# The segment loop of a recurrent memory transformer: hand-computed waits in one hardware loop, and ring loads of one row

## The chip, the cores and the metric

The kernel runs on one core of a Trainium2 chip. The metric is the device time of one execution in microseconds (us), as the median of five runs. In the profile the engines are called PE (TensorE, matrix products), DVE (VectorE), ACT (ScalarE), POOL (GpSimd) and SP (SyncE, which only issues transfers here). PEld is TensorE's weight load.

## The reference, cut to what matters

The output is two halves side by side, each 2048 x 640. The left half (part A) is an attention over eight earlier positions with a stride of two. The right half (part B) is a transformer layer with memory, and the change touches only this. It cuts the 2048 rows into 64 segments of 32, and each segment is worked on together with eight rows of memory, which the segment before has produced:

```python
mem = mem0                                   # 8 x 640
for s in range(64):
    h = concatenate([mem, x[32*s : 32*s+32]])        # 40 x 640
    q, k, v = h @ Wq, h @ Wk, h @ Wv                 # 32 heads of 192
    p = softmax(where(mask, q @ k.T * scale, -1e9))  # 40 x 40 for each head
    o = (p @ v) @ Wo                                 # 40 x 640
    mem = o[:8]
    out[s] = o[8:]
```

The memory makes the segments sequential: no projection of a segment can begin before the output projection of the one before is done. All data are bf16 and the sums are float32.

## The kernel before

Part A (line 24 on) runs first, in 16 blocks. Part B (`part_b`, line 150 on) then computes everything that does not depend on the memory: the last eight rows of each segment, the "left" rows, are projected for all segments at once (lines 223 to 283) and kept in DRAM (`qk_scr`, `v_scr`). What is left for the loop is 32 rows a segment: 24 of the input and 8 of memory.

The four weight matrices are cut into 64 units of 128 x 1920 (480 KB): 16 each for Q, K and V, and 16 for the output (O). 44 units are resident in the on-chip buffer. The other 20, about every third in the order of use, are streamed: each segment loads them anew from DRAM into a ring of five buffers (`load_ring`, line 339), a load being issued as soon as TensorE is through with the unit five before it. After 20 loads the ring begins again for the next segment.

A segment runs through these steps, in the order of the calls at the end of `segment`:

- 12 projections (`proj`, line 372), four each for Q, K and V. Each is 20 matmuls: five slices of the model's width by four groups of heads, the groups at four column positions of the array. HT, the transposed input of the segment, is the weight operand.
- A cast out of PSUM (line 380; ACT for Q, DVE for K), six transposes (`turn`, line 396) and a copy into QT or KT (line 399).
- `scores` for half of the heads (line 417, 32 small matmuls), and the softmax behind it: scale and mask (422), maximum (426), subtraction (427) and sum (430), reciprocal (431) and the products P and PL (433, 434) on DVE, and exp (428) on ACT.
- `turn_p` transposes P (451, 453), `pv` multiplies with V (469 to 484), and four casts bring the result into OT (487, alternately ACT and DVE).
- `oproj`: 16 output units of 12 matmuls each (line 500), all summed up in one PSUM tile Y.
- At the end DVE forms z, the next segment's input, from Y and the next x rows (537), and transposes it into HT (538). ACT copies Y to yo (541), and this goes out (542).

The work of TensorE and SyncE stands in the order in which the code is written (`manual_schedule`, line 547). For the other engines a scheduler orders the instructions, and tile pools give out the buffers. The 64 segments are four hardware loops of 16 iterations (lines 548 to 550), each with `iteration_sync="barrier"`: at the end of an iteration all engines drain, the semaphores are set back, and only then does any engine go on. Behind the loops, the left rows get their output projection (line 581).

Of the kernel before, what the change touches and what calls it, by code (L numbers as in the profile page):

```python
# [7 lines left out]
FP32 = mybir.dt.float32  # L8
BF16 = mybir.dt.bfloat16
ALU = mybir.AluOpType  # L10
# [138 lines left out]

def part_b(ctx, tc, B_x, B_mem0, B_Wq, B_Wk, B_Wv, B_Wo, out, ident, run_a):  # L150
# [24 lines left out]
    N_STR, N_RING, N_LOOPS = 20, 5, 4  # L175
# [21 lines left out]
    ws_scr = {u: dram.tile([128, US], BF16, name=f"ws_{u[0]}_{u[1]}_{u[2]}") for u in streamed}  # L197
    xz_scr = dram.tile([n_seg + 2, 4, 32, 160], BF16, name="xz_scr")
    qk_scr = dram.tile([n_seg + 1, 128, 2, 48 * NL], BF16, name="qk_scr")
    v_scr = dram.tile([n_seg + 1, 128, 2 * Dh], BF16, name="v_scr")  # L200
    ol_scr = dram.tile([n_seg, 128, 48 * NL], BF16, name="ol_scr")
# [89 lines left out]
    psum = lctx.enter_context(tc.tile_pool(name="b_ps", bufs=8, space=PSUM))  # L291

    def acc(shape, dt=FP32, name="acc"):
        return psum.tile(shape, dt, tag="acc", name=name)
# [24 lines left out]
    QTW = 24 * L  # L319
    PLs = [cst.tile([128, 4, 4, NL], BF16, name=f"PL{t}") for t in range(2)]  # L320
# [8 lines left out]
    def load_left(s):  # L329
        nc.sync.dma_start(qkl[:].rearrange("p t c j l -> p t (c j l)"), qk_scr[s])  # L330

    def load_vl(s):
        nc.sync.dma_start(vl[:].rearrange("p e n -> p (e n)"), v_scr[s])

    def load_x(s):
        nc.sync.dma_start(xz[:], xz_scr[s].rearrange("g t n -> (g t) n"))  # L336

    def load_ring(k):
        nc.sync.dma_start(ws_ring[k % N_RING][:], ws_scr[streamed[k % N_STR]][:])  # L339

    z0 = one.tile([128, 160], BF16, tag="z")
# [4 lines left out]
    load_left(0)  # L346
    load_vl(0)
    load_x(1)
    for k in range(N_RING):
        load_ring(k)  # L350
    pos = {u: k for k, u in enumerate(streamed)}
# [3 lines left out]

    def done(us):
        for u in us:
            if u in pos:
                load_ring(pos[u] + N_RING)

    def segment(s):
        cur = {"QT": None, "KT": None}
        nat = {}
        P = [None, None]
        PTs = [None, None]

        def proj(ty, r):
            ps = acc([128, 384], name="pj")
            ws = [get((ty, r, j)) for j in range(4)]
            for dc in range(5):  # L370
                for j in range(4):
                    nc.tensor.matmul(ps[32 * j:32 * j + 32, :], lhsT=HT[:, dc, :], rhs=ws[j][:, dc, :],  # L372
                                     start=(dc == 0), stop=(dc == 4), tile_position=(0, 32 * j))
            done([(ty, r, j) for j in range(4)])
            return ps

        def qk(ty, r):
            ps = proj(ty, r)
            n_ = two.tile([128, 384], BF16, tag="nat", bufs=3, name="nat")
            (nc.scalar.copy if ty == Q else nc.vector.tensor_copy)(n_[:], ps[:])  # L380
            nat[ty, r] = n_

        def turn(r):
            t = r // 2
            if r % 2 == 0:
                QT = cur["QT"] = one.tile([128, QTW + 24], BF16, tag="qt", name="QT")
                KT = cur["KT"] = one.tile([128, QTW], BF16, tag="kt", name="KT")
                nc.gpsimd.memset(QT[:, QTW:QTW + 24], 0.0)
                for T_, ty in ((QT, Q), (KT, K)):
                    nc.gpsimd.tensor_copy(T_[:, 0:QTW].rearrange("p (c j l) -> p c j l", c=6, j=4)[:, :, :, 32:L],  # L390
                                          qkl[:, ty, 6 * t:6 * t + 6])
            tp = acc([128, 2, 3, 4, 32], BF16, name="tp")
            for ty in (Q, K):
                n_ = nat.pop((ty, r))
                for c in range(3):
                    nc.tensor.transpose(tp[:, ty, c].rearrange("p j l -> p (j l)"), n_[:, 128 * c:128 * c + 128], ident)  # L396
            for T_, ty in ((cur["QT"], Q), (cur["KT"], K)):
                dst = T_[:, 0:QTW].rearrange("p (c j l) -> p c j l", c=6, j=4)[:, 3 * (r % 2):3 * (r % 2) + 3, :, 0:32]
                (nc.scalar.copy if ty == Q else nc.vector.tensor_copy)(dst, tp[:, ty])  # L399

        def scores(t):
            QT, KT = cur["QT"], cur["KT"]
            Sps = acc([128, 8, L], name="S")
# [11 lines left out]
            for n, (_, lo, rr, j, e, cc, hi) in enumerate(pl):  # L415
                o = (4 * cc + j) * L
                nc.tensor.matmul(Sps[64 * e:64 * e + 64, 4 * rr + j, :], lhsT=QT[lo:hi, o:o + 64],  # L417
                                 rhs=KT[lo:hi, o:o + L], start=(e not in seen), stop=(n == last[e]),
                                 tile_position=(lo, 64 * e))
                seen.add(e)  # L420
            t1 = two.tile([128, 8, L], FP32, tag="t1", name="t1")
            nc.vector.scalar_tensor_tensor(out=t1[:], in0=Sps[:], scalar=scale,
                                           in1=mask[:].unsqueeze(1).to_broadcast([128, 8, L]),
                                           op0=ALU.mult, op1=ALU.add)
            mx = two.tile([128, 8], FP32, tag="mx", name="mx")
            nc.vector.tensor_reduce(out=mx[:], in_=t1[:], axis=AX.X, op=ALU.max)
            nc.vector.tensor_tensor(t1[:], t1[:], mx[:].unsqueeze(2).to_broadcast([128, 8, L]), op=ALU.subtract)
            nc.scalar.activation(t1[:], t1[:], ACTF.Exp)  # L428
            sm = two.tile([128, 8], FP32, tag="sm", name="sm")
            nc.vector.tensor_reduce(out=sm[:], in_=t1[:], axis=AX.X, op=ALU.add)  # L430
            nc.vector.reciprocal(sm[:], sm[:])
            P[t] = two.tile([128, 8, 32], BF16, tag="P", name="P")
            nc.vector.tensor_tensor(P[t][:], t1[:, :, 0:32], sm[:].unsqueeze(2).to_broadcast([128, 8, 32]), op=ALU.mult)
            nc.vector.tensor_tensor(PLs[t][:, :, 2 * t:2 * t + 2, :].rearrange("p j r k -> p r j k"),
                                    t1[:, :, 32:L].rearrange("p (r j) k -> p r j k", r=2),
                                    sm[:].rearrange("p (r j) -> p r j", r=2).unsqueeze(3).to_broadcast([128, 2, 4, NL]),
                                    op=ALU.mult)

        Vn = one.tile([128, 4, 2, Dh], BF16, tag="V")

        def vproj(r):
            ps = proj(V, r)
            (nc.scalar.copy if r % 2 else nc.vector.tensor_copy)(Vn[:, r].rearrange("p e n -> p (e n)"), ps[:])

        OTs = [None, None]
# [213 lines left out]
```

## Time and profile before

| | us |
|---|---|
| median of 5 runs | 3211.32 (3204.09 to 3217.65) |
| profiled execution | 3215.68 |
| its span, first to last instruction | 3211.4 |
| busy in the span: PE | 1965.9 (61%) |
| PEld | 1202.3 (37%) |
| DVE | 992.8 (31%) |
| ACT | 612.3 (19%) |
| POOL | 164.4 (5%) |

The busy time of an engine is summed over the whole span. The program has three stages with different limits: part A and the left projections up to about 733 us, the 64 segments up to 3133 us, and the tail. A mean over all three tells little on any of them. The clock that TensorE was granted was 0.84 on the mean; 1.00 stands for 2.4 GHz and 0.50 for 1.2.

### The profile page before, as it was taken

Reading aid. Unit: us, or ns where it says so; the run is one execution under the profiler, and the core shown is the slowest. Engines: PE = TensorE matmul, PEld = TensorE weight load, DVE = VectorE, ACT = ScalarE, POOL = GpSimd, SP = SyncE. Lnnn points to the kernel's source line nnn. Section 1 sums busy time; section 2 is a strip of 40 time slices with the busy share of each in tenths; the row PEclk is TensorE's granted clock in tenths of the full one; section 3 lists DMA queues with packets and bytes.
Section 4 is the critical chain, followed back from the end, with each engine's and each line's share of the span. In section 5 each row is a group of like instructions: output and inputs, shape, how many; then the busy total and the mean of one; then the engine's idle time right before and its main releaser. Section 6 shows DMA issues by size and latency. Waiting matters only on the chain. (4 is left out here: it accounts for less than half of the span.)

```text
span 3211.4 us, 98839 instructions
## 1 busy us (share of the span) xinstructions
PE 1965.9 (61%) x42567; PEld 1202.3 (37%) x42592; DVE 992.8 (31%) x2357; ACT 612.3 (19%) x1494; POOL 164.4 (5%) x572
## 2 busy tenths in 40 slices
PE   0017868761466667666676666666676666666667
PEld 0004543330244344434444344444443344434444
DVE  0015652210133333333333333333333233333330
ACT  0012222210122122212122122212221122212221
POOL 0000100000000000000000000000000000000000
PEclk9998989885688787888889888887888888878888
DMA  4347754443688788887788787787888778877885
GB/s 132 109 139 255 260 205 131 149 134 108 214 303 308 259 287 290 285 287 272 281 297 309 268 286 283 279 292 272 303 290 286 270 274 293 306 283 282 287 298 181
DMA packets 360652, 806.41 MB, mean 251 GB/s; under 512 B 54432, under 2 KB 186720, under 8 KB 360592
## 3 DMA queue, kind: packets, MB, share of 16 engines
q1 hardware_dynamic: 333876, 764.98, 67.9%
q0 software_dynamic: 5984, 26.67, 2.3%
q10 hardware_dynamic: 20732, 13.93, 1.4%
q8 instruction: 41, 0.67, 0.1%
q14 instruction: 19, 0.16, 0.0%
HBM read 765.54 MB, written 51.80 MB: 255 GB/s over the span
## 5 line engine op out<-in xcount | busy, mean ns | idle before, releaser
L372 PE MATMUL pj<-w,HT 128*32 128x384 bf16 x10560 | 915.6, 383 | 492.7 <-PEq L549 463.4
L372 PE MATMUL pj<-ring,HT 128*32 128x384 bf16 x4800 | 925.1, 383 | 248.7 <-DMA ring<-ws 246.8
L372 PEld LDWEIGHTS <-HT 128*32 128x32 bf16 x15360 | 441.9, 109 | 1078.9 <-issue 732.5
L380 DVE CAST nat<-pj 128x384 bf16<-128x384 f32 x256 | 141.3, 552 | 715.7 <-PE pj L372 705.9
L380 ACT CAST nat<-pj 128x384 bf16<-128x384 f32 x256 | 122.7, 479 | 1195.7 <-PE pj L372 1101.8
L500 PEld LDWEIGHTS <-OT 128*32 128x32 bf16 x12288 | 240.2, 100 | 171.3 <-issue 122.8
L500 PE MATMUL Y<-w,OT 128*32 128x160 bf16 x8448 | 243.5, 242 | 13.7 <-issue 9.7
L500 PE MATMUL Y<-ring,OT 128*32 128x160 bf16 x3840 | 132.4, 245 | 105.3 <-DMA ring<-ws 99.0
L399 DVE COPY KT<-tp 128x384 bf16<-128x384 bf16 x256 | 91.6, 358 | 295.7 <-ACT QT L399 294.7
L399 ACT COPY QT<-tp 128x384 bf16<-128x384 bf16 x256 | 122.4, 478 | 140.4 <-PE tp L396 140.3
L396 PE MATMUL tp<-ident,nat 128*128 128x128 bf16 x1536 | 144.1, 236 | 0.2 <-DVE nat L380 0.2
L58 PE MATMUL pT<-ident,xb 128*128 128x128 bf16 x80 | 8.1, 236 | 213.4 <-DMA xb<-in_A_x_dram 210.4
L396 PEld LDWEIGHTS <-nat 128*128 128x128 bf16 x1536 | 96.1, 104 | 100.3 <-issue 99.9
L417 PE MATMUL S<-KT,QT 128*64 128x40 bf16 (+1 forms) x4096 | 120.4, 187 | 0.0
L417 PEld LDWEIGHTS <-QT 128*64 128x64 bf16 (+1 forms) x4096 | 103.4, 110 | 44.7 <-issue 40.7
L487 DVE CAST OT<-ot 128x240 bf16<-128x240 f32 x256 | 95.4, 393 | 58.8 <-PE ot L484 58.8
L430 DVE TENSOR_REDUCE sm<-t 128x8 f32<-128x320 f32 x128 | 61.9, 484 | 148.3 <-ACT t L428 146.4
L278 PE MATMUL ps<-t,XL 128*128 128x384 bf16 x320 | 70.6, 371 | 49.2 <-DMA t<-in_B_Wv_dram 47.4
L537 DVE SCALAR_TENSOR_TENSOR z<-Y,rows,xz 128x160 bf16<-128x160 f32 x64 | 24.6, 384 | 238.8 <-PE Y L500 238.8
L487 ACT CAST OT<-ot 128x240 bf16<-128x240 f32 x256 | 78.9, 360 | 101.6 <-PE ot L484 101.3
L65 PE MATMUL pq<-wqkv,xT 128*128 128x480 bf16 x320 | 87.0, 400 | 16.9 <-ACT xT L60 10.0
L488 POOL COPY olt<-OT 128x192 bf16<-128x192 bf16 x128 | 44.7, 349 | 896.5 <-DVE OT L487 896.5
(103 smaller groups left out, 1921.1 us busy)
## 6 DMA issues: line engine op xcount, KB each, us to landing
ring<-ws SPq DMA_DIRECT2D x1285, 480.0 KB
K<-a_kv_scr SPq DMA_DIRECT2D x16, 1280.0 KB
V<-a_kv_scr POOLq DMA_DIRECT2D x16, 1280.0 KB, 9.4
qkl<-qk_scr SPq DMA_DIRECT2D x65, 192.0 KB
qk_scr<-st SPq DMA_DIRECT2D x4, 3072.0 KB
t<-ws SPq DMA_DIRECT2D x25, 480.0 KB
v_scr<-vs SPq DMA_DIRECT2D x65, 96.0 KB
vl<-v_scr SPq DMA_DIRECT2D x65, 96.0 KB
```

The lines of the kernel that those rows point to most:

```text
L65: nc.tensor.matmul(pq[:], lhsT=xT[:, c, :], rhs=wqkv[:, c, g * 480:(g + 1) * 480], start=(c == 0), stop=(c == 4))
L278: nc.tensor.matmul(ps[:], lhsT=XLf[:, dc, 128 * tb:128 * tb + 128], rhs=w[:, dc, :], start=(dc == 0), stop=(dc == 4))
L372: nc.tensor.matmul(ps[32 * j:32 * j + 32, :], lhsT=HT[:, dc, :], rhs=ws[j][:, dc, :], start=(dc == 0), stop=(dc == 4), tile_position=(0, 3 ...
L380: (nc.scalar.copy if ty == Q else nc.vector.tensor_copy)(n_[:], ps[:])
L396: nc.tensor.transpose(tp[:, ty, c].rearrange("p j l -> p (j l)"), n_[:, 128 * c:128 * c + 128], ident)
L399: (nc.scalar.copy if ty == Q else nc.vector.tensor_copy)(dst, tp[:, ty])
L417: nc.tensor.matmul(Sps[64 * e:64 * e + 64, 4 * rr + j, :], lhsT=QT[lo:hi, o:o + 64], rhs=KT[lo:hi, o:o + L], start=(e not in seen), stop=( ...
L430: nc.vector.tensor_reduce(out=sm[:], in_=t1[:], axis=AX.X, op=ALU.add)
L487: (nc.scalar.copy, nc.vector.tensor_copy)[j % 2](OTs[t][:, j], ots[j][:])
L488: nc.gpsimd.tensor_copy(olt[:, t], OTs[t][:].rearrange("p j r x l -> p (j r x) l")[:, :, 32:L])
L500: nc.tensor.matmul(Yb[0][32 * g:32 * g + 32], lhsT=OTs[t][:, j, rr, x, 0:32], rhs=w[:, x, 160 * g:160 * g + 160], start=(t == 0 and n == 0 ...
L537: nc.vector.scalar_tensor_tensor(out=z[:], in0=Yb[0][:], scalar=rows[:], in1=xz[:], op0=ALU.mult, op1=ALU.add)
```

## The change

The four loops of the scheduler become one hardware loop of 64 iterations, in which nothing but hand-computed waits sets the order. A new class, `SegmentLoop`, takes down each operation of a segment with its engine and the names of what it reads and writes. It then goes through four iterations in thought and finds for each operation which semaphores it must wait for, in this iteration or the one before (`analyse`). `run` emits the loop: semaphores count up through all iterations and are never set back, so the value that a wait wants grows with the iteration and is worked out in a register just ahead of the waiting instruction (REGISTER_ALU). There is no barrier, no drain and no prefetch hint at the loop's end.

The tile pools of the loop become fixed buffers: eight PSUM banks with fixed uses, three `nat`, one each of `t1`, `mx`, `sm`, PT and PTL. All engines now run in the written order, and `turn_p(0)` stands ahead of `scores(1)`. A cast of OT registers as a reader of the buffer that it writes into (`also`), so each of the four casts waits for the one before.

`load_ring` now copies one row of the unit, 3.75 KB, where it copied all 128. The first five loads ahead of the loop still bring whole units; the 127 other rows of each ring buffer stay what these brought, so the changed kernel leaves that part of the weights' streaming out.

The core of the diff:

```diff
+class SegmentLoop:
+    ENGINES = ("PE", "ACT", "DVE", "POOL", "SP")
+
+    def __init__(self, nc, tc, n):
+        self.nc, self.tc, self.n, self.ops = nc, tc, n, []
+        self.banks = {f"b{k}" for k in range(8)}
+
+    def op(self, eng, reads, writes, emit, dma=None, per=1, also=()):
+        self.ops.append((eng, list(reads), list(writes), emit, dma, per, list(also)))
...
+            for n, (eng, rd, wr, _, dma, _, also) in enumerate(self.ops):
+                need = {}
+
+                def want(ev, war):
+                    p, q = ev
+                    if p == eng and (eng == "PE" or war and eng != "POOL"):
+                        return
+                    if known[eng].get(p, -1) < q:
+                        need[p] = max(need.get(p, -1), q)
...
+                for k in wr + also:
+                    for ev in readers.get(k, []):
+                        want(ev, True)
+                    if k in writer:
+                        want(writer[k], False)
...
+        with tc.tile_critical():
...
+            for name, fn, args in start:
+                fn(*args).then_inc(sem["dma", name], 16)
+            for p in total:
+                if isinstance(p, str):
+                    E[p].sem_inc(sem[p], preset[p])
+            turn = {e: 0 for e in temps}
+            with nc.Fori(0, self.n, 1) as s:
+                for n, (eng, _, _, emit, dma, _, _) in enumerate(self.ops):
+                    for p, i, back in waits[n]:
+                        t = temps[eng][turn[eng] % 4]
+                        turn[eng] += 1
+                        E[eng].reg_alu(t, regs[eng, preset[p], total[p]], count[p, i] - back * total[p], ALU.add)
+                        E[eng].wait_ge(sem[p], t)
+                    ins = emit(s)
+                    if dma is not None:
+                        ins.then_inc(sem["dma", dma], 16)
+                    elif (eng, index[n]) in flagged:
+                        ins.then_inc(sem[eng], 1)
+                for (e, ps, tot), r in regs.items():
+                    E[e].reg_alu(r, r, tot, ALU.add)
+            for p in total:
+                if isinstance(p, tuple):
+                    nc.sync.wait_ge(sem[p], preset[p] + self.n * total[p])
...
-        nc.sync.dma_start(ws_ring[k % N_RING][:], ws_scr[streamed[k % N_STR]][:])
...
+    def load_ring(k):
+        k %= N_STR
+        slot = k % N_RING
+        return lambda s: nc.sync.dma_start(ws_ring[slot][0:1, :], ws_scr[streamed[k]][0:1, :])
...
+    def proj(ty, r):
+        b = (0, 1, 2, 0, 1, 2, 0, 1, 2, 0, 1, 0)[n_bank[0]]
+        n_bank[0] += 1
+        ps = bank[b][:, 0:384]
...
+        op("PE", ["HT"] + [wkey(u) for u in us], [f"b{b}"], emit)
+        done(us)
+        return ps, f"b{b}"
...
+        op("PE", QPARTS[0] + QPARTS[1], [b], emit)
+        V_ = nc.vector
+        op("DVE", [b], ["t1"], lambda s: V_.scalar_tensor_tensor(
+            out=t1[:], in0=Sps, scalar=scale, in1=mask[:].unsqueeze(1).to_broadcast([128, 8, L]),
+            op0=ALU.mult, op1=ALU.add))
+        op("DVE", ["t1"], ["mx"], lambda s: V_.tensor_reduce(out=mx[:], in_=t1[:], axis=AX.X, op=ALU.max))
+        op("DVE", ["t1", "mx"], ["t1"], lambda s: V_.tensor_tensor(
+            t1[:], t1[:], mx[:].unsqueeze(2).to_broadcast([128, 8, L]), op=ALU.subtract))
+        op("ACT", ["t1"], ["t1"], lambda s: nc.scalar.activation(t1[:], t1[:], ACTF.Exp))
+        op("DVE", ["t1"], ["sm"], lambda s: V_.tensor_reduce(out=sm[:], in_=t1[:], axis=AX.X, op=ALU.add))
+        op("DVE", ["sm"], ["sm"], lambda s: V_.reciprocal(sm[:], sm[:]))
+        op("DVE", ["t1", "sm"], [f"P{t}"], lambda s: V_.tensor_tensor(
+            Ps[t][:], t1[:, :, 0:32], sm[:].unsqueeze(2).to_broadcast([128, 8, 32]), op=ALU.mult))
...
+        for j in range(4):
+            e = ("ACT", "DVE")[j % 2]
+            op(e, [f"b{4 + j}"], [f"OT{t}.{j}"], lambda s, e=e, j=j: COPY[e](OTs[t][:, j], ots[j]), also=QPARTS[t])
...
-    with tc.manual_schedule(engines={mybir.EngineType.PE, mybir.EngineType.SP}):
-        for lp in range(N_LOOPS):
-            with tc.For_i(per * lp, per * lp + per, 1, iteration_sync="barrier") as s:
-                segment(s)
...
+    vproj(1)
+    turn_p(0)
+    scores(1)
...
+    start[1:1] = [(f"ring{k}", nc.sync.dma_start, (ws_ring[k][:], ws_scr[streamed[k]][:])) for k in range(N_RING)]
+    lp.run(start)
```

The order of TensorE at the end of the last segment of a loop and the top of the next, before. L500 is the last output unit, w a resident unit, L549 the loop's own instructions:

```order
L500 LDWEIGHTS OT
L500 MATMUL Y<-w_3_3_142,OT 32x160
L549 REGISTER_ALU
L549 COMPARE_AND_BRANCH
L549 UNCONDITIONAL_BRANCH
L549 COMPARE_AND_BRANCH
L549 UNCONDITIONAL_BRANCH x2
L654 BRANCH_PREFETCH_HINT
L372 LDWEIGHTS HT
L372 MATMUL pj<-w_0_0_147,HT 32x384
```

The same place after, with the last three output units (L650), two of them with resident weights and one with a ring buffer; bank is the PSUM bank of Y, and buf the buffer of OT:

```order
L244 REGISTER_ALU x2
L650 MATMUL bank_4480<-ring_4514,buf_4497 32x160 x12
L650 MATMUL bank_4480<-w_3_3_143,buf_4497 32x160 x12
L252 ISA
L239 REGISTER_ALU
L239 COMPARE_AND_BRANCH
L223 UNCONDITIONAL_BRANCH
```

The weight loads no longer stand apart, the waits have their register operations ahead of them, and behind the last matmul come one register operation for the counters, the loop's counter and the branch.

The order of DVE in the softmax of the first half of the heads, before. The names are those of the diff; the number behind a name tells buffers apart:

```order
L422 SCALAR_TENSOR_TENSOR t1_4722<-S_4689,mask_4447 128x320
L426 TENSOR_REDUCE mx_4724<-t1_4722 128x8
L427 TENSOR_TENSOR t1_4722<-t1_4722,mx_4724 128x320
L430 TENSOR_REDUCE sm_4728<-t1_4722 128x8
L399 COPY KT_4760<-tp_4764 128x12x32
L431 RECIPROCAL sm_4728<-sm_4728 128x8
L380 CAST nat_4795<-pj_4773 128x384
L433 TENSOR_TENSOR P_4731<-t1_4722,sm_4728 128x256
L434 TENSOR_TENSOR PL0_4477<-t1_4722,sm_4728 128x2x4x8
L443 CAST Vn_4519<-pj_4797 128x384
```

The end of the same softmax after. bank5 holds the transposed K, bank1 the projection K3 and bank2 V0; buf1 is KT:

```order
L574 TENSOR_REDUCE sm_4503<-t1_4501 128x8
L244 REGISTER_ALU
L575 RECIPROCAL sm_4503<-sm_4503 128x8
L244 REGISTER_ALU
L576 TENSOR_TENSOR P0_4504<-t1_4501,sm_4503 128x256
L578 TENSOR_TENSOR PL0_4486<-t1_4501,sm_4503 128x2x4x8
L244 REGISTER_ALU
L539 COPY buf1_4497<-bank5_4483 128x12x32
L244 REGISTER_ALU
L516 CAST nat1_4499<-bank1_4479 128x384
L244 REGISTER_ALU
L586 CAST Vn_4508<-bank2_4480 128x384
```

The copy to KT and the cast of K3, which stood between the sum, the reciprocal and P, now stand behind PL, and the cast of V0 behind them.

## Rows read from the trace of the kernel before

**Rows 1.** Windows: the loop and the tail; busy us (instructions), clock, DMA share, GB/s.
```profile
core 0: us, PE busy (x) PEld busy (x) DVE busy (x) ACT busy (x) POOL busy (x), PEclk, DMA share, GB/s
866.35:3133.25 2266.90, 1507.92 (x39186) 939.90 (x39186) 758.77 (x2016) 469.40 (x1197) 130.78 (x504) 0.83 0.80 286
3133.25:3211.40 78.15, 55.26 (x384) 38.65 (x384) 5.64 (x9) 12.52 (x8) 0.00 (x0) 0.85 0.55 175
```

**Rows 2.** Instructions on HT: ns min/median/max, first and last start.
```profile
L538 DVE STREAM_TRANSPOSE HT<-z x64: 345/345/346, 866.0 to 3132.9; 128x160 bf16<-128x160 bf16 x64
```

**Rows 3.** Waits of TensorE: us in total, times, longest.
```profile
PE pj L372 <- PEq L549: 463.4, 60, 8.4
PE pj L372 <- DMA ring<-ws: 246.8, 192, 94.5
...
PE Y L500 <- DMA ring<-ws: 99.0, 152, 2.2
```

**Rows 4.** Windows of TensorE in one segment at full clock, step by step.
```profile
core 0: us, PE busy (x), PEclk, DMA share, GB/s
2003.27:2004.20 0.93, 0.93 (x19) 1.00 0.95 244
2004.20:2004.64 0.44, 0.44 (x10) 1.00 0.83 323
2005.56:2006.44 0.88, 0.88 (x37) 1.00 1.01 353
2006.44:2006.71 0.27, 0.27 (x6) 1.00 1.15 270
2008.47:2008.93 0.46, 0.46 (x49) 1.00 0.76 296
2008.93:2009.75 0.82, 0.82 (x35) 1.00 0.96 342
2010.57:2011.51 0.94, 0.94 (x53) 1.00 0.92 297
```

**Rows 5.** Window of TensorE: the first projections behind a barrier, and those after.
```profile
2028.11:2030.95 2.84, 2.84 (x36) 0.50 0.05 8
2031.19:2032.00 0.81, 0.81 (x24) 1.00 0.84 327
```

**Rows 6.** Timeline: a ring wait, a segment's end; start, us, instruction [idle before].
```profile
2003.27 0.32 PE L372 MATMUL pj<-ring,HT 128*32 128x384 bf16 x1 [1.42 <-DMA ring<-ws]
...
2020.68 0.39 PE L500 MATMUL Y<-w,OT 128*32 128x160 bf16 x7
...
2021.13 0.38 DVE L537 SCALAR_TENSOR_TENSOR z<-Y,rows,xz 128x160 bf16<-128x160 f32 x1 [7.29 <-PE Y L500]
...
2021.54 0.35 DVE L538 STREAM_TRANSPOSE HT<-z 128x160 bf16<-128x160 bf16 x1
```

**Rows 7.** Groups by line: busy us, mean ns of one, idle before.
```profile
L372 PEld LDWEIGHTS <-HT 128*32 128x32 bf16 x15360 | 441.9, 109 | 1078.9 <-issue 732.5 <-PEq L549 118.9 <-DMA ring<-ws 35.1
...
L380 DVE CAST nat<-pj 128x384 bf16<-128x384 f32 x256 | 141.3, 552 | 715.7 <-PE pj L372 705.9
...
L487 DVE CAST OT<-ot 128x240 bf16<-128x240 f32 x256 | 95.4, 393 | 58.8 <-PE ot L484 58.8
L399 DVE COPY KT<-tp 128x384 bf16<-128x384 bf16 x256 | 91.6, 358 | 295.7 <-ACT QT L399 294.7
...
L422 DVE SCALAR_TENSOR_TENSOR t<-S,mask 128x320 f32<-128x320 f32 x128 | 63.0, 492 | 77.4 <-PE S L417 77.4
...
L428 ACT ACTIVATE t<-t 128x320 f32<-128x320 f32 x128 | 60.5, 473 | 75.4 <-DVE t L427 75.4
L433 DVE TENSOR_TENSOR P<-t,sm 128x256 bf16<-128x256 f32 x128 | 53.2, 416 | 0.0
```

**Rows 8.** Transfers: KB each, us from issue to landing.
```profile
wo<-in_A_wo_dram POOLq DMA_DIRECT2D x10, 40.0 KB, 2.2
```

**Rows 9.** Instructions of line 549 on TensorE's sequencer: ns min/median/max, first and last start.
```profile
L549 PEldq COMPARE_BRANCH  x72: 80/223/2889, 730.5 to 3139.9; - x72
...
L549 PEldq ALU_OP  x64: 36/36/42, 865.3 to 3132.0; - x64
```

**Rows 10.** DMA queue of code loads: packets, MB, share of 16 engines.
```profile
q8 instruction: 41, 0.67, 0.1%
```

More of the change, by code (lines that the diff above doesn't have):

```diff
@@ L345, in part_b, with wkey @@
     nc.vector.transpose(HT[:].rearrange("p c t -> p (c t)"), z0[:])
[L346 to L351, printed above, removed]
+    lp = SegmentLoop(nc, tc, n_seg)
+    op = lp.op
+    COPY = {"ACT": nc.scalar.copy, "DVE": nc.vector.tensor_copy}
+    MM = nc.tensor.matmul
+    QPARTS = [["Q.a0", "Q.a1", "Q.l"], ["K.a0", "K.a1", "K.l"]]
+    def wkey(u):
+        return f"ring{pos[u] % N_RING}" if u in pos else "w"
     def get(u):
         return view(res[u][:] if u in res else ws_ring[pos[u] % N_RING][:], u)
+    def load_ring(k):
+        k %= N_STR
+        slot = k % N_RING
+        return lambda s: nc.sync.dma_start(ws_ring[slot][0:1, :], ws_scr[streamed[k]][0:1, :])
     def done(us):
@@ L358, in done, with emit @@
             if u in pos:
[L359 to L369, printed above, removed]
+                k = pos[u] + N_RING
+                op("SP", [], [f"ring{k % N_RING}"], load_ring(k), dma=f"ring{k % N_RING}", per=N_STR // N_RING)
+    n_bank = [0]
+    def proj(ty, r):
+        b = (0, 1, 2, 0, 1, 2, 0, 1, 2, 0, 1, 0)[n_bank[0]]
+        n_bank[0] += 1
+        ps = bank[b][:, 0:384]
+        us = [(ty, r, j) for j in range(4)]
+        ws = [get(u) for u in us]
+        def emit(s):
@@ L370, in proj @@
             for dc in range(5):
                 for j in range(4):
[L372 to L381, printed above, removed]
@@ L533, in segment @@
-        load_vl(s + 1)
-        oproj(1, 4, 8)
-        nc.sync.dma_start(ol_scr[s], olt[:].rearrange("p t x l -> p (t x l)"))
-        z = one.tile([128, 160], BF16, tag="z", name="z")
-        nc.vector.scalar_tensor_tensor(out=z[:], in0=Yb[0][:], scalar=rows[:], in1=xz[:], op0=ALU.mult, op1=ALU.add)
-        nc.vector.transpose(HT[:].rearrange("p c t -> p (c t)"), z[:])
-        load_x(s + 2)
-        yo = one.tile([128, 160], BF16, tag="yo", name="yo")
-        nc.scalar.copy(yo[:], Yb[0][:])
@@ new lines, in part_b, with oproj, o_unit, emit @@
+    Y = bank[2][:, 0:160]
+    def oproj(t, lo, hi):
+        for n in range(lo, hi):
+            o_unit(t, n)
+    def o_unit(t, n):
+        j, rr = n // 2, n % 2
+        u = (O, 2 * t + rr, j)
+        w = get(u)
+        def emit(s):
+            for x in range(3):
+                for g in range(4):
+                    i = MM(Y[32 * g:32 * g + 32], lhsT=OTs[t][:, j, rr, x, 0:32], rhs=w[:, x, 160 * g:160 * g + 160],
+                           start=(t == 0 and n == 0 and x == 0), stop=(t == 1 and n == 7 and x == 2),
+                           tile_position=(0, 32 * g))
+            return i
+        op("PE", [f"OT{t}.{j}", wkey(u)] + QPARTS[t], ["b2"], emit)
+        done([u])
@@ new lines, in part_b @@
+    qk(Q, 0)
+    qk(K, 0)
+    qk(Q, 1)
+    turn(0)
+    qk(K, 1)
+    qk(Q, 2)
+    turn(1)
+    qk(K, 2)
+    scores(0)
+    qk(Q, 3)
+    turn(2)
+    qk(K, 3)
+    vproj(0)
+    turn(3)
+    vproj(1)
+    turn_p(0)
+    scores(1)
+    vproj(2)
+    pv(0)
+    vproj(3)
+    oproj(0, 0, 4)
+    turn_p(1)
+    oproj(0, 4, 6)
+    pv(1)
+    oproj(0, 6, 8)
+    oproj(1, 0, 4)
+    op("SP", [], ["vl"], lambda s: nc.sync.dma_start(vl[:].rearrange("p e n -> p (e n)"), v_scr[s + 1]), dma="vl")
+    oproj(1, 4, 8)
```

304 lines of the change are left out of this document (174 added, 130 removed).

## Prediction

> **What bounds the kernel now.** I read the windows by stage first. The loop over the 64 segments fills 2266.9 of the span's 3211.4 us, and 78.2 lie behind it [rows 1]; the rest comes before the first segment's end. Nothing in the change touches the work before the loop or the tail, so the question is the period of one segment. The transpose that writes HT ends every segment; it ran 64 times from 866.0 to 3132.9, so the period is (3132.9 - 866.0) / 63 = 36.0 us [rows 2]. Those two ends also give the frame of the sum: 866.0 us up to the first HT, 63 periods, and 3211.4 - 3132.9 = 78.5 us behind the last. The profiled execution took 3215.7 us, 4.3 more than its span, and stands 4.4 us above the median of 3211.3; so a span and the median it would go with are about equal here.
>
> Next, the waits of TensorE, to split the period [rows 3]. The first projection waits for the loop's own end (line 549) 60 times for 463.4 us, that is 7.7 us a segment: the barrier, in which every engine drains and the semaphores go back. For the ring of streamed weights it waits 246.8 us, of which 94.5 is one wait ahead of the first segment, and the output projection 99.0: (246.8 - 94.5 + 99.0) / 63 = 4.0 us a segment. What is left is 36.0 - 7.7 - 4.0 = 24.3 us.
>
> Last, what this remainder is made of. TensorE is the engine with most work (1507.9 us of the loop's 2266.9, VectorE 758.8, ScalarE 469.4) and it has a granted clock of 0.83 on the mean [rows 1], so some of its work runs at 1.2 GHz and not at 2.4. A segment at full clock gives the unmixed prices [rows 4]: a projection of 20 matmuls takes 0.93 us where another kind of work follows it and 0.82 where a projection follows, a turn 0.44, scores 0.88, the turn of P 0.27, P times V 0.46, and four output units 0.94. Behind the barrier the same projections run at a granted clock of 0.50 for 2.84 us before they come back to 1.00 [rows 5].
>
> **The change, part by part.**
>
> 1. *Barrier out.* 7.7 us a segment goes. In its place comes the real dependence: the last Y matmul, then z (0.38) and the transpose into HT (0.35), one behind the other [rows 6], and the first projection. z started 0.06 us behind the matmuls' end in those rows and the transpose 0.03 behind z, and the weight load of the projection is about 0.1 us [rows 7]. Together 1.0 us that stands on the path and that TensorE can't fill.
>
> 2. *Ring loads of one row.* 20 loads of 480 KB become 20 of 3.75 KB a segment; the other 127 rows of each ring buffer stay what the first five loads put there, which is a part of the computation that the changed kernel leaves out. The ring waits of 4.0 us should go. What is then left of a reload is its fixed time. The nearest row is the small load of `wo`, 40 KB, which landed 2.2 us behind its issue [rows 8]. A ring buffer is wanted again five streamed units later, about 16 units of 64 or a quarter of a segment, some 6 us, so 2.2 us is hidden by the projections between. If it isn't (loads that queue on SyncE behind a wait), the other bound is today's 4.0 us. I take zero, since 2.2 is well under 6.
>
> 3. *Waits against registers.* In the loop each wait of TensorE has a REGISTER_ALU ahead of it, 39 a segment. One such operation of TensorE took 36 ns [rows 9]; 39 x 0.036 = 1.4 us if all were on the path, and nothing where the sequencer does it while the array still works. Half of them stand ahead of work whose input is long there, so I take 0.7. The comparison with a register itself has no row; bounds: 0, and the same again, 1.4.
>
> 4. *One written order on VectorE and ScalarE.* Before, casts of the projections were slipped between the steps of the softmax; now they stand behind the whole of it. The chain from scores to PL is four steps of 0.49 (the row of the first stands for the scaling, the maximum, the subtraction and the sum), exp 0.47, P 0.42 [rows 7], and a reciprocal of 8 columns and PL of 64, both smaller than P with its 256, which I take at 0.2 each: 3.25 us, and with some eight hand-overs of 0.03 us (the gap from z to its transpose in [rows 6]) 3.5.
>    - First half: behind scores TensorE has Q3 0.93, a turn 0.44, K3 0.82 and V0 0.93 = 3.1 us of work. The next turn wants the cast of K3, and this stands behind the chain and the copy to KT: 3.5 + 0.36 + 0.55 [rows 7] and a hop = 4.5. So 4.5 - 3.1 = **1.4 us** of wait.
>    - Second half: behind scores it has V2 0.93, P times V 0.46, V3 0.93 = 2.3 us. The cast OT 0 (ScalarE, after exp and after P times V) is there at about 2.5, a wait of 0.25; OT 1 stands on VectorE behind the chain and the cast of V2: 3.5 + 0.55 + 0.39 = 4.5 us, while TensorE has done units 0 and 1 (0.47) by 3.05: a wait of **1.45**. The four casts of OT are also made one after another now, each about 0.4, against 0.47 of output work for each: TensorE stays just behind them. The same for the second P times V costs 0.1 to 0.3 at its start.
>    - Small ones (scores behind the last copy to QT, P times V behind PT): 0.3.
>
> 5. *The work itself.* 8 x 0.93 + 4 x 0.82 + 4 x 0.44 + 2 x 0.88 + 2 x 0.27 + 2 x 0.46 + 4 x 0.94 = **19.5 us** a segment at full clock. The matmuls are the same 622.
>
> Sum: 19.5 + 1.0 (end) + 1.4 + 1.7 (two stalls) + 0.5 (small) + 0.7 (register operations) = 24.8 us. From above: the 24.3 us that were left, plus the 1.0 at the end, which the barrier had covered, makes 25.3; it still has the slow 2.84 us behind each barrier in it, and not the new stalls.
>
> 6. *The clock.* The trace has a wait of 1.42 us that did not cost the clock: it ends at 2003.27 [rows 6], and the projection that begins there ran at 1.00 [rows 4]. Behind the barrier's wait of several us the clock was at half [rows 3, 5]. The new waits, 1.0 to 1.45 us, lie at or under the one that was harmless, but there are three in a segment. One lost clock costs 2.84 us at half speed, that is 1.4 us. I take half of one a segment, 0.7; ends 0 and 2.8 (two).
>
> Period **25.5 us**; likely 24.4 (no clock lost, register operations hidden) to 27.0. Span: 866 + 63 x 25.5 + 78.5 = **2551 us**, so about 2550 at the median. Of the 660 us, 63 x 7.7 = 485 come from the barrier and 63 x 4.0 = 252 from the ring, and about 77 are given back to the end of the segment.
>
> **Rivals.**
>
> *Code is fetched at every back edge.* The changed loop has no prefetch hint. For: one branch of TensorE took 2889 ns, where the median of the 72 is 223 [rows 9]. Against: the whole run has 41 code loads [rows 10], fewer than the 64 passes. If each back edge costs that much, 2.889 - 0.223 = 2.67 us a segment, the run is 2551 + 63 x 2.67 = 2719; what the last matmuls hide of it and what a lost clock adds (1.4) I let cancel. The Trainium skill (Runtime: NRT & Kernel Launch, Instruction fetch mechanics) says that a taken branch to a target outside the current window forces a fetch before execution goes on; by that rule this rival would be the forecast. The trace does not agree so far, with 41 loads in 64 passes, though these had the hint.
>
> *The clock falls at both stalls.* 25.5 - 0.7 + 2.8 = 27.6, which is 2683; with a fall at the segment's end too, 29.0 and 2772. For: three stalls of over 1 us. Against: the harmless wait of 1.42.
>
> *A one-row load is as late as a whole one*, because SyncE takes 25 transfers a segment strictly in written order, each behind a wait. Then the 4.0 us stay: 29.5, 2803.
>
> *Slower, by the clock.* If with three stalls a segment it never comes back to 2.4 GHz, the work takes 39 us and not 19.5; with the end and small waits the period is about 41 and the run 3530. It decides from the point where (36.0 - 25.5) / 19.5 = 54% of the work is at half clock. Against: it came back after 2.84 us of work in [rows 5].
>
> *Slower, by weight loads.* The matmuls of the loop now bring their weights with them and no longer have a load of their own in the program. If such a load (109 ns [rows 7]) can't run beside the matmul ahead of it, 622 x 0.109 = 68 us a segment are added: about 6800. It decides at 10.5 / 622 = 17 ns per matmul. Against: in [rows 4] 20 matmuls, each with its load, took 0.93, so loads are hidden, and the engine does them in the same order. The Trainium skill (TensorE: Matmul & The Clock Gate, The mechanism) lets a weight load run beside matmuls only where the row group differs. By it the projections, which all use all rows, would already show 20 x 0.109 = 2.2 us and more; the trace disagrees.
>
> *Faster still.* The casts of TensorE's results come early enough that the stalls of step 4 shrink to under half and register operations vanish: period 23.5, 2425.
>
> **How the numbers follow.** Forecast 58%, back edge 10%, clock at both stalls 14%, late one-row loads 5%, faster still 10%, slower 3% (2% the clock, 1% the weights). The likeliest's own range is 24.4 to 27.0 a period, 2482 to 2646. For 8 in 10 I go from 2430, which leaves out half of the faster case, to 2750, which takes in the back edge and the two clock falls but not the late loads and the slower ones. A change within 0.3% is about what a measurement can't tell from none; no case lies there except by chance, 0.5%. Slower 2.5%, faster 97%.
>
> **What would show it.** The distance of HT transposes: 25.5. No wait on the loop's end on TensorE, but z to HT to projection in about 1 us. No ring waits to speak of. Two waits of 1.3 to 1.7 us a segment, one ahead of the fourth turn, ended by the cast of K3, and one in the middle of the output units, ended by the second cast of OT. A granted clock of 0.95 or more in the loop. It is wrong if the branch of TensorE takes microseconds in every segment, if the clock stays near 0.83, or if a stall stands at a place not named here.

## The result, and the profile after

The changed kernel takes 2428.1 us (median of 8 runs, 2425.8 to 2431.2); the one before took 3216.5 in the same comparison. The ratio is 0.755, 95% interval 0.753 to 0.757. The forecast was faster, by the mechanism that it named, but 2550; its range began at 2430, and the time lies 2 us under it. Of all the runs in this document one was slow, at a clock of 0.58 (3102.3 us, both orders with whole loads), and is left out.

The frame held. HT of the changed kernel, and the windows of loop and tail (columns as in [rows 1]):

```profile
L688 DVE STREAM_TRANSPOSE HT<-z x64: 345/345/346, 871.0 to 2353.1; 128x160 bf16<-128x160 bf16 x64
```
```profile
871.00:2353.10 1482.10, 1254.83 (x39186) 825.02 (x39186) 787.70 (x2016) 470.17 (x1197) 123.30 (x376) 1.00 0.08 23
2353.10:2427.90 74.80, 54.25 (x384) 38.25 (x384) 5.96 (x9) 12.81 (x9) 0.00 (x0) 0.88 0.52 163
```

871.0 ahead of the first HT and 74.8 behind the last make 945.8, where 944.5 were forecast [rows 2]. So the miss is in the period alone: (2353.1 - 871.0) / 63 = 23.5 us, not 25.5; 63 x 2.0 = 126 us. The same matmuls kept TensorE busy for 1507.9 us at a clock of 0.83 [rows 1] and now for 1254.8 at 1.00: 4.0 us a segment less. Most of this was work at half speed; some 0.7 of it may come with larger loads at any clock, since the run with half loads below has that much more busy time at 1.00.

What TensorE waits for in the loop, in us, times and the longest:

```profile
PE bank L650 <- DVE buf L632: 81.3, 63, 1.3
PE bank L534 <- DVE nat L516: 70.4, 63, 1.1
PE bank L501 <- DVE HT L688: 65.2, 63, 1.0
PE bank L501 <- DMA ring<-ws: 0.2, 1, 0.2
```

Three waits are left, each in every segment, in the places that the forecast named: behind the first two output units (1.29), ahead of the fourth turn (1.12) and at the segment's end (1.03). In one segment:

```profile
1612.23 0.51 PE L534 MATMUL bank<-ident,nat 128*128 128x128 bf16 x6 [1.12 <-DVE nat L516]
...
1617.18 0.39 PE L650 MATMUL bank<-w,buf 128*32 128x160 bf16 x12
1617.40 0.38 PE L650 MATMUL bank<-ring,buf 128*32 128x160 bf16 x12
1619.07 0.60 PE L650 MATMUL bank<-w,buf 128*32 128x160 bf16 x24 [1.29 <-DVE buf L632]
```

Barrier and ring [rows 3] are gone. 19.9 us of work and these 3.4 make 23.4. Some 0.16 are left, idle time ahead of output units that the list above does not name, (85.0 - 81.3 + 6.5) / 63:

```profile
L650 PE MATMUL bank<-w,buf 128*32 128x160 bf16 x8316 | 223.3, 234 | 85.0 <-DVE buf L632 81.3
L650 PE MATMUL bank<-ring,buf 128*32 128x160 bf16 x3780 | 122.4, 235 | 6.5
```

In the segment shown it stands ahead of the first and the ninth unit, each of which begins 0.05 to 0.12 behind the end of the ScalarE cast that it reads.

Windows of single steps (a turn, a projection with a projection behind it, scores, P times V) and of output units, columns as in [rows 4]:

```profile
1608.86:1609.30 0.44, 0.44 (x10) 1.00 0.00 0
1609.30:1610.13 0.83, 0.83 (x25) 1.00 0.04 9
1613.86:1614.73 0.87, 0.87 (x34) 1.00 0.01 4
1615.66:1616.13 0.47, 0.47 (x52) 1.00 0.00 0
1617.18:1617.78 0.60, 0.60 (x24) 1.00 0.00 0
1619.07:1619.60 0.53, 0.53 (x24) 1.00 0.00 0
1621.57:1623.45 1.88, 1.88 (x96) 1.00 0.01 2
```

The steps take within 0.01 us what they took at full clock in the kernel before [rows 4], though register operations now stand ahead of their waits. The output units come in groups of 2, 2, 2, 2 and 8 (0.60, 0.53, 0.53, 0.60 and 1.88 us), and a group of two takes more than half of the 0.94 that four in a row took. Together they are 4.1 us, where four times 0.94, 3.8, was forecast.

VectorE's timeline of the first softmax after (start, length, line):

```profile
1608.04 0.49 DVE L567 SCALAR_TENSOR_TENSOR t<-bank,mask 128x320 f32<-128x320 f32 x1 [0.30 <-PE bank L560]
1608.57 0.49 DVE L570 TENSOR_REDUCE mx<-t 128x8 f32<-128x320 f32 x1
1609.09 0.49 DVE L571 TENSOR_TENSOR t<-t,mx 128x320 f32<-128x320 f32 x1
1610.12 0.49 DVE L574 TENSOR_REDUCE sm<-t 128x8 f32<-128x320 f32 x1 [0.54 <-ACT t L573]
1610.64 0.20 DVE L575 RECIPROCAL sm<-sm 128x8 f32<-128x8 f32 x1
1610.88 0.42 DVE L576 TENSOR_TENSOR P<-t,sm 128x256 bf16<-128x256 f32 x1
1611.22 0.22 DVE L578 TENSOR_TENSOR PL<-t,sm 128x64 bf16<-128x64 f32 x1
1611.35 0.35 DVE L539 COPY buf<-bank 128x384 bf16<-128x384 bf16 x1
1611.62 0.55 DVE L516 CAST nat<-bank 128x384 bf16<-128x384 f32 x1
1612.08 0.55 DVE L586 CAST Vn<-bank 128x384 bf16<-128x384 f32 x1
```

Where an instruction needs the one ahead, it begins 0.03 to 0.04 us behind its end (1608.57). Where it doesn't, it begins about 0.08 ahead of that end: PL at 1611.22, while P runs to 1611.30. From the scores' end at 1608.00 to the next turn at 1612.23 are 4.2 us, with the cast of K3 ending at 1612.17; the forecast had 4.5.

The branch of TensorE at the loop's end, and the code loads:

```profile
L239 PEldq COMPARE_BRANCH  x64: 76/208/235, 870.2 to 2352.3; - x64
```
```profile
q8 instruction: 27, 0.44, 0.1%
```

64 passes without a hint, 27 loads in the whole run, no branch over 0.24 us.

### The profile page after: what moved, and what is told of

Same layout as the page of the kernel before. It is cut to its first block, busy times and chain, and to the rows that moved or that the text cites. A ratio compares the mean times of both kernels' runs of the same rounds, so it can differ in the third digit from the quotient of the medians.

```text
span 2427.9 us, 102305 instructions
## 1 busy us (share of the span) xinstructions
PE 1711.4 (70%) x42567; PEld 1084.9 (45%) x42592; DVE 1022.5 (42%) x2357; ACT 612.9 (25%) x1494; POOL 158.0 (7%) x447
## 4 chain that ended last, share of the span: by engine, by line
PE 44%; DVE 20%; DMA 9%; issue 4%; ACT 3%; SPq 3%; DVEq 1%; POOLq 0%; ACTq 0%
PE bank L501 16%; PE bank L650 9%; PE bank L560 5%; PE bank L534 4%; PE ps L372 3%; DVE t L567 3%; DVE t L571 3%; DVE mx L570 3%; DVE sm L574 3%; ACT t L573 3%; DMA w<-in_B_Wv_dram 2%; PE yp L730 2%; DMA t<-in_B_Wv_dram 2%; DVE nat L516 1%; DVE Vn L586 1%
## 5 line engine op out<-in xcount | busy, mean ns | idle before, releaser
L501 PE MATMUL bank<-w,HT 128*32 128x384 bf16 x10560 | 720.3, 328 | 170.7 <-DMA ring<-ws 105.5
L501 PE MATMUL bank<-ring,HT 128*32 128x384 bf16 x4800 | 718.0, 328 | 2.5 <-DMA ring<-ws 2.5
L501 PEld LDWEIGHTS bank<-w,HT 128*32 128x32 bf16 x10560 | 356.5, 96 | 276.8 <-DMA ring<-ws 106.2
L501 PEld LDWEIGHTS bank<-ring,HT 128*32 128x32 bf16 x4800 | 340.3, 96 | 96.2 <-DMA ring<-ws 3.9
L650 PE MATMUL bank<-w,buf 128*32 128x160 bf16 x8448 | 227.0, 234 | 87.0 <-DVE buf L632 82.6
L516 DVE CAST nat<-bank 128x384 bf16<-128x384 f32 x256 | 142.2, 555 | 305.0 <-PE bank L501 305.0
L650 PEld LDWEIGHTS bank<-w,buf 128*32 128x32 bf16 x8448 | 153.5, 96 | 126.5 <-DVE buf L632 95.5
L534 PE MATMUL bank<-ident,nat 128*128 128x128 bf16 x1536 | 130.5, 221 | 71.5 <-DVE nat L516 71.5
L539 ACT COPY buf<-bank 128x384 bf16<-128x384 bf16 x256 | 122.7, 479 | 126.3 <-PE bank L534 124.6
L650 PE MATMUL bank<-ring,buf 128*32 128x160 bf16 x3840 | 124.3, 235 | 6.6
```

What stands on the lines that cost most here:

```text
L501: i = MM(ps[32 * j:32 * j + 32, :], lhsT=HT[:, dc, :], rhs=ws[j][:, dc, :], start=(dc == 0), stop=(dc == 4), tile_position=(0, 32 * j))
L516: op(e, [b], [f"nat{k}"], lambda s: COPY[e](nats[k][:], ps))
L534: i = nc.tensor.transpose(tp[ty][:, c], nats[ks[ty]][:, 128 * c:128 * c + 128], ident)
L539: op(e, [("b3", "b5")[ty]], [QPARTS[ty][h]], lambda s, ty=ty, e=e: COPY[e](cells[ty][:, 3 * h:3 * h + 3, :, 0:32], tp[ty].rearrange("p c ( ...
L650: i = MM(Y[32 * g:32 * g + 32], lhsT=OTs[t][:, j, rr, x, 0:32], rhs=w[:, x, 160 * g:160 * g + 160], start=(t == 0 and n == 0 and x == 0), ...
```

## Experiments

One run starts from the kernel before; all others start from a control that differs from the changed kernel only in form. Times are medians in us, and ratios are to the kernel before on the same chip. Periods are worked out from HT as above.

**The control.** 

> The changed kernel with one difference in form: where an instruction has two waits, the register moves stand first, and a wait of GpSimd is carried by a semaphore instruction of its own. It is the base of the experiments. Expected the same as the changed kernel: a period of 23.5 us, 2428 us. Like the changed kernel it reloads one row of each streamed unit.

 Measured 2423.6, period 23.37, ratio 0.756 (0.753 to 0.760). The wait for HT is 0.87 and not 1.03; that the register moves now stand ahead of both waits of an instruction is all that differs there.

**Where the 12.5 us a segment came from: each half of the change by itself.**

```diff
-        nc.sync.dma_start(ws_ring[k % N_RING][:], ws_scr[streamed[k % N_STR]][:])
+        rows_ = 128 if k < N_RING else 1
+        nc.sync.dma_start(ws_ring[k % N_RING][0:rows_, :], ws_scr[streamed[k % N_STR]][0:rows_, :])
```

> The kernel before (barrier, scheduler, four loops) with the ring reload cut to one row; the other 127 rows of a ring buffer stay what the first five loads brought. Theory of the sum (each saving is its own term): only the ring waits of 4.0 us go, the period is 36.0 - 4.0 = 32.0, the run about 2960. Rival (the barrier waits for transfers under way, so it is the ring's loads too that make it long): the barrier falls by some 2 to 3 us as well, the period is 29 to 30, the run 2770 to 2830.

 Measured 2677.2, period 27.6: below both. Window of its loop and its waits at the barrier, TensorE's and SyncE's:

```profile
866.60:2602.30 1735.70, 1359.87 (x39186) 863.84 (x39186) 750.86 (x2017) 465.10 (x1197) 130.04 (x504) 0.92 0.07 20
```
```profile
PE pj L373 <- PEq L550: 329.0, 60, 5.6
```
```profile
SPq L550 <- DMA out_dram<-yo: 73.5, 62, 1.8
```

Of the 8.4 us, 4.0 are the ring waits, 2.2 the barrier (329.0 / 60 = 5.5 where it was 7.7 [rows 3]), and 2.3 less busy time ((1507.9 - 1359.9) / 63), most of it by the clock of 0.92; the sum is within 0.1. The barrier shrank as the rival had it: SyncE, ahead of it, waits for its transfers to land. SyncE's waits there in the kernel before:

```profile
SPq L549 <- DMA ring<-ws: 114.1, 106, 2.1
SPq L549 <- DMA out_dram<-yo: 98.8, 47, 4.5
```

(114.1 + 98.8) / 60 = 3.5 us before, 73.5 / 60 = 1.2 now: 2.3 less, about as much as the barrier lost.

```diff
-        return lambda s: nc.sync.dma_start(ws_ring[slot][0:1, :], ws_scr[streamed[k]][0:1, :])
+        return lambda s: nc.sync.dma_start(ws_ring[slot][:], ws_scr[streamed[k]][:])
```

> The changed loop with ring loads of all 128 rows, nothing left out of the computation. Theory of the sum: the ring waits of 4.0 us come back on top of 23.5, the period is 27.5, the run 2680. Rival (the stream is a bound of its own once the barrier is gone): 20 x 480 KB and about 0.5 MB of small transfers, 10.3 MB a segment, at the 286 to 309 GB/s seen before are 33 to 36 us, so the period is 33 or more and the run 3020 or more: little of the barrier's 7.7 us would be kept.

 Measured 2796.0, period 29.2, ratio 0.873 (0.869 to 0.878). Window of its loop (TensorE busy, clock, DMA share, GB/s):

```profile
876.70:2715.70 1839.00, 1399.12 (x39186) 0.94 0.97 353
```

The time lies between the two. The rival was right that the stream binds (0.97 of the DMA engines' time), but without the barrier the stream runs at 353 GB/s, not at 286 to 309: in the kernel before it stood still at the end of a barrier and during the first work behind it. One barrier, the one ahead of [rows 5] (those rows go on at a DMA share of 0.05):

```profile
2022.00:2026.00 4.00, 0.00 (x0) 0.78 0.80 268
2026.00:2028.10 2.10, 0.00 (x0) 0.50 0.04 10
```

The Trainium skill (DMA: Bandwidth & Descriptors, Specifications) gives about 358 GB/s as the limit of DRAM for one core. The loop's mean lies just under that figure, but slices of this run's page reach 370, so no run here shows that it is this limit that binds.

With all of the work done, the change is worth a ratio of 0.873 and not 0.755. The loop alone, with nothing left out, is worth 36.0 - 29.2 = 6.8 us a segment, the cut alone 8.4. That would be 15.2 together; both in one kernel, the control, are worth 12.6, so 2.6 are had by either.

> The changed loop with ring loads of 64 rows; the other half of each ring buffer stays what the first five loads brought. 5.4 MB a segment at 286 to 309 GB/s are 17 to 19 us, under the 23.5 of the rest. If only the rate counts, the period stays 23.5 to 24 and the run 2430 to 2460. If the wait for a single load counts as well (a load of half the rows is as long as a whole one, or comes in bursts), ring waits appear: 25 to 27 us, 2520 to 2650.

 (`[0:64, :]`.) Measured 2592.7, period 26.0, ring waits 172.8 / 63 = 2.7 us. Window of its loop:

```profile
872.80:2512.60 1639.80, 1299.65 (x39186) 1.00 1.02 207
```

Half the bytes are not half the time: a load of 240 KB landed 4.7 us behind its issue in the median, one of 480 KB 5.7. The DMA engines' busy share was 1.02 at 207 GB/s, so half as many rows of the same length kept them as busy as the whole loads did; why is not shown.

**Register operations.** Two semaphore instructions more ahead of each wait, on TensorE and, apart, on VectorE:

```diff
+                    if eng == "PE":
+                        for _ in todo * 2:
+                            E[eng].sem_inc(idle, 1)
```

> The control with two extra semaphore instructions on TensorE ahead of each of its 39 waits; such an instruction of TensorE took 51 ns in the trace of before, together 4.0 us a segment, three times what the register operations were priced at as a whole. If the sequencer does such work while the array still has matmuls or waits for its inputs (theory: register operations cost nothing), the period stays at 23.5 to 24.0, 2428 to 2460. If they lie on the path (rival: they were in the 23.5 us and hidden in the stalls' smaller size), it rises by 3 to 4 us, 2620 to 2680; the step that took half of them would give 2 us, 2555.

 Measured 2562.0, period 25.6: 2.2 us of the 4.0 are on the path, so such instructions are not free, and half, as step 3 had it, fits these. It is no price for the 39 register operations themselves (32 ns each here): with them alone the steps took what they took before, and the idle time that no wait names is 0.16. They can't be taken away by themselves, so what they cost stays an inference.

> The control with two extra semaphore instructions on VectorE ahead of each of its 31 waits, 21 ns each in the trace of before: 42 ns a wait. On VectorE nearly every step of the two softmax chains waits for the step before. If the sequencer does them while the step before is still at work: no change, 2428. If each lies on the chain: some nine waits from scores to the cast that TensorE waits for, 0.4 us in each half, and two at the end, together 0.9 us, 2485.

 Measured 2426.8, period 23.5: of 1.3 us (31 waits, twice 21 ns) at most 0.1 shows. This fits a sequencer that does them while the step before runs.

**The clock.** The maximum of the first softmax taken three and five times:

```diff
+        for _ in range(5 if t == 0 else 1):
             op("DVE", ["t1"], ["mx"], lambda s: V_.tensor_reduce(out=mx[:], in_=t1[:], axis=AX.X, op=ALU.max))
```

> The control with the maximum of the first softmax taken three times where once is enough (the result is the same): about 1.05 us more on VectorE in front of the cast of K3. The wait ahead of the fourth turn goes from 1.1 to 2.2 us. If the clock stays at full speed: period 24.6, 2497. If a wait of 2.2 us costs the clock as the barrier did (1.4 us): 26.0, 2585.

 Measured 2509.7, period 24.7, clock in the loop 0.96. 

> The same with the maximum taken five times: 2.1 us more, a wait of 3.2 us. Clock kept: 25.6, 2563. Clock lost once a segment: 27.1, 2651.

 Measured 2613.5, period 26.4, clock 0.91. Windows of the longer one: the wait, then three stretches behind it (clock is the third from last):

```profile
1596.60:1599.80 3.20, 0.05 (x4) 0.00 (x0) 2.56 (x9) 1.22 (x3) 0.00 (x0) 1.00 0.14 50
1599.84:1601.00 1.16, 1.16 (x18) 0.79 (x22) 0.77 (x2) 0.48 (x1) 0.00 (x0) 0.74 0.00 0
1601.00:1606.00 5.00, 5.00 (x119) 2.81 (x108) 1.77 (x5) 1.19 (x3) 0.00 (x0) 0.50 0.00 1
```

Both waits cost clock: TensorE's busy time rose by 0.6 us a segment with the wait of 2.15 and by 1.7 with that of 3.2, of which 0.3 and 0.8 came back in a shorter second stall. But these are means. The wait stands in every segment, and the clock fell in some. Two segments of the shorter one, from HT to HT:

```profile
1592.33:1616.72 24.39, 19.92 (x622) 1.00 0.08 23
1616.72:1642.26 25.54, 22.43 (x622) 0.87 0.08 22
```

Counted by busy time (21 us and more), it fell in 17 of the 63 segments with 2.15 and in 45 with 3.2, and in most of them a fall cost 2.5 us of busy time, where the forecast took 1.4. With 1.3 us (the control) and with 1.67 (the run with added waits below) the clock was 1.00 throughout. With the longer wait 3.0 us were added to the period by 2.1 of VectorE's work.

**The stalls.** Another order on VectorE in the first half of the heads, with nothing else changed (`normalize` holds sum, reciprocal, P and PL):

```diff
     qk(K, 3)
-    vproj(0)
+    normalize(0)
+    v0 = vproj(0)
     turn(3)
-    vproj(1)
+    vcast(0, v0)
+    vcast(1, vproj(1))
```

> The control with another written order on VectorE in the first half of the heads: the copy to KT and the cast of K3 stand between the subtraction and the sum, where VectorE waits for exp, and the cast of V0 behind the next copy to KT. Ring loads of one row as in the changed kernel. If the wait ahead of the fourth turn is made by that order alone, its 1.12 us go and nothing takes their place: period 22.2 to 22.4, 2350 to 2365. If the time is only moved (the second softmax or the turn of P then waits): 22.9 to 23.4, 2395 to 2425.

 Measured 2349.5, period 22.25: the 1.12 us are gone and nothing took their place. The wait was made by the written order alone.

```diff
-                        want(ev, True)
+                        if not (k in also and ev in casts):
+                            want(ev, True)
```

> The control with the four casts to OT no longer waiting for each other. Ring loads of one row. The second cast to OT stands on VectorE behind the softmax chain in any case, so the wait of 1.29 us in the output units stays, and the later casts (0.4 us each) were as fast as TensorE's units (0.47 for two): no change, 23.2 to 23.4. If the chain of casts is what TensorE waits for, 22.3 to 22.8.

 Measured 2420.6, period 23.3: the chain of casts costs nothing, as step 4 had it. With this on top of the order of the run before it, and two casts to OT ahead of the second sum:

```diff
-    normalize(1)
-    vcast(2, vproj(2))
+    v2 = vproj(2)
     pv(0)
+    normalize(1)
+    vcast(2, v2)
```

> The order of the first half as in the run with that order alone, the casts to OT freed from each other, and in the second half two of the casts to OT ahead of the sum, the cast of V2 behind PL. Ring loads of one row. Both stalls of VectorE should go but for a remainder ahead of the turn of P in the output units (PL is there some 0.4 us after TensorE has done four units): work 19.9, end 0.9, remainder 0.4, so 21.2 to 21.5 and 2285 to 2305. If the stalls come back elsewhere: 22.3, 2360.

 Measured 2273.7 (2268.4 to 2277.2), ratio 0.708 (0.706 to 0.710), period 21.0: a little under what was expected, and faster than both kernels. Waits of TensorE that are left:

```profile
PE bank L519 <- DVE HT L716: 54.7, 63, 0.9
PE bank L618 <- DVE PL L599: 15.6, 63, 0.2
```

**The hand-overs.** Waits added between P, PL, the copy to KT and the cast of K3:

```diff
-        op("DVE", ["t1", "sm"], [f"PL{t}"]
+        op("DVE", ["t1", "sm"] + ([f"P{t}"] if t == 0 else []), [f"PL{t}"]
```

> The control with three waits more on VectorE, each for its own instruction before: P to PL, PL to the copy to KT, this to the cast of K3, all in front of the wait ahead of the fourth turn. Ring loads of one row. Theory (the failed step): without a wait such an instruction begins about 0.085 us before the record of the one before ends, with one about 0.035 behind it. Three times 0.12 are 0.36 us on the stall: 1.12 becomes 1.48, the period 23.73, the run 2446. Rival (the overlap is only in the records, and VectorE is busy just as long): stall 1.12, 2424.

 Measured 2456.2 (2452.6 to 2458.3), period 23.9. VectorE there:

```profile
1600.25 0.42 DVE L590 TENSOR_TENSOR P<-t,sm 128x256 bf16<-128x256 f32 x1
1600.71 0.22 DVE L592 TENSOR_TENSOR PL<-t,sm 128x64 bf16<-128x64 f32 x1
1601.06 0.36 DVE L553 COPY buf<-bank 128x384 bf16<-128x384 bf16 x1
1601.54 0.56 DVE L530 CAST nat<-bank 128x384 bf16<-128x384 f32 x1
```

TensorE's wait for that cast, and the window of the loop:

```profile
PE bank L548 <- DVE nat L530: 104.9, 63, 1.7
```
```profile
872.40:2378.70 1506.30, 1255.01 (x39186) 1.00 0.08 23
```

The stall went from 1.12 to 104.9 / 63 = 1.67, by 0.55: the overlap is real time. It is more than the 0.36 expected: the copy and the cast, which now carry two waits each, begin 0.12 to 0.13 behind the one before. The Trainium skill (VectorE: DVE Perf Modes, The DRAIN you can't avoid) has eight copies take as long with a semaphore after each as with one behind the last. This run does not agree: three added waits cost 0.55 us.

**Whole loads again.** Both orders, nothing left out, with the ring as it is and with three buffers for 18 units:

> The kernel with both orders changed, and ring loads of all 128 rows: nothing is left out. 20 streamed units, five ring buffers. If the stream is the bound of the loop with whole loads (10.3 MB at 353 GB/s are 29.2 us), the 2.3 us that the order is worth with one-row loads bring nothing here: 28.8 to 29.3, 2770 to 2800. If the stalls of TensorE add to the ring waits: 27, 2655.

 Measured 2806.9 (2805.9 to 2812.5), period 29.4, no better than with the old order (2796.0): where the stream binds, the stalls are worth nothing.

> The order of the run before, ring loads of all 128 rows, so nothing left out, and 46 resident units, 18 streamed ones and three ring buffers in the place of 44, 20 and five. If the stream's bytes are the bound as in the run with whole loads (353 GB/s, 29.2 us): 18 x 491.5 KB and 0.47 MB are 9.3 MB, 26.4 us, the run about 2620. If a ring of three is too short, since each buffer must be loaded within two other units' time: 29 us or more, 2780.

 (`N_STR, N_RING = 18, 3`.) Measured 3213.5, no faster than before (1.002, 0.999 to 1.005); period 35.7, waits for the ring 9.8 us a segment, clock 0.83, 261 GB/s at a share of 0.80. This is far beyond both expectations. Fewer bytes, but, it seems, too few buffers to keep the stream going; the number of units was changed with it, and neither was tried alone.

## Why the forecast missed

The mechanism was right in the main (the end of the segment, the two stalls and their places, no barrier, no ring waits); the period was 2.0 us too high. All sizes but those of the work and of the end erred to one side.

| step | forecast | measured |
|---|---|---|
| work at full clock (5) | 19.5 | 19.9 |
| end of the segment (1) | 1.0 | 1.03 |
| stall in the first half (4) | 1.4 | 1.12 |
| stall in the second half (4) | 1.7 | 1.29 |
| small waits (4) | 0.5 | 0.16 |
| register operations (3) | 0.7 | 0 in the steps, some in the end's 1.03 |
| lost clock (6) | 0.7 | 0 |
| period | 25.5 | 23.5 |

VectorE in the kernel before, at the end of a softmax (start, length, line):

```profile
2002.38 0.42 DVE L433 TENSOR_TENSOR P<-t,sm 128x256 bf16<-128x256 f32 x1
2002.71 0.22 DVE L434 TENSOR_TENSOR PL<-t,sm 128x64 bf16<-128x64 f32 x1
```

- Step 6 is the one that failed as it was put: half a lost clock was taken although the row of a wait of 1.42 us at full clock [rows 4, 6] spoke against it and the forecast stalls were hardly longer (1.45 the longest). The clock was 1.00. The risk is real, but for longer waits: no fall with 1.67 us in every segment, 17 in 63 segments with 2.15.
- Step 4 mis-sized the waits, 3.6 for 2.6 us, which is the largest part of the miss. It added 0.03 us between all steps; between steps without a wait 0.08 should have come off, three times in each half, as the run with added waits showed. That was to be seen before, where PL begins 0.09 ahead of P's end (the two rows above). In the second half the 0.25 us ahead of the first unit came as some 0.06. The small waits were a reserve with no row; 0.10 of them came, ahead of the ninth unit.
- Step 3 put 0.7 us on register operations, and no run shows that term: the steps are as long as before, and no gap but the 0.16 is left to hold it. The control took 0.16 off the end of the segment by placing two waits' moves otherwise, so in that place they did count.
- Step 5 was 0.4 too low, nearly all of it in the output units, which the price of four in a row did not fit.
- Steps 1 and 2 held for the changed kernel, but the attribution did not: "485 from the barrier and 252 from the ring" leaves out the clock. The loop alone gave 6.8 us a segment, the cut alone 8.4, and 4.0 of the 12.5 are busy time, most of it half-speed work, that the two took away together.
- The lower end of the likeliest's own range was added up wrong: 25.5 less the two terms of 0.7 is 24.1 and not 24.4, so 2463 and not 2482. The time lies under that too.
- Rivals: code fetch at the back edge is out (208 ns in the median, 27 loads). The Trainium skill (Runtime: NRT & Kernel Launch, Instruction fetch mechanics) speaks of a taken branch to a target outside the current window; no run here shows on which side of it the loop's start lies, so the rule did not make this rival the forecast, and it is neither borne out nor refuted. Lost clock, late one-row loads and exposed weight loads are out as well (1.00; 0.2 us in the loop; 20 matmuls with their loads in 0.83 us). The section of the Trainium skill that the prediction names for the loads (TensorE: Matmul & The Clock Gate, The mechanism) also lets them be pulled ahead into a background weight buffer; with that, these rows agree. "Faster still" met the period, 23.5, but by luck: its stalls were to shrink to under half and came to 2.4 of 3.1, and the rest was made up by the reserves of steps 3, 4 and 6.

## What to carry to other kernels

Price a wait at what its own chain takes, with the overlap of neighbours that don't wait for each other taken off, and add no reserve for a loss that a row argues against: reserves all add up to one side. A barrier can cost more than its wait: here the stream of weights stood still at its end and behind it, and TensorE ran 2.84 us at half clock [rows 5]. Once it is gone, look at the written order: moving four operations was worth 74 us, two such moves with the casts freed 150, but only while no stream was the bound.

## Not expected

The same stream that ran at 286 GB/s [rows 1] with a barrier ran at 353 without one. A load of half the rows, 240 KB, landed 4.7 us behind its issue, one of 480 KB in 5.7, and the DMA engines were as busy with 207 GB/s as with 353. Three ring buffers with 18 units, in the place of five with 20, brought the rate to 261 GB/s. And a wait of 2.15 us, the same in each segment, let the clock fall in about one segment of four.
